# A Fourier mixing layer and a capacity-limited mixture of experts on one core: row gathers in another order with a third buffer, running sums in PSUM, scatters declared independent, two selection rounds fewer, and loads on another queue

## The chip, the cores and the metric

One core of a Trainium2 chip. The metric is device time in microseconds (us) of one execution; of several executions the median is given. Engines: TensorE (PE: matmuls; PEld: its weight loads), VectorE (DVE), ScalarE (ACT), GpSimd (POOL) and SyncE (SP). SP, ScalarE and GpSimd each have a queue on which they issue DMAs.

## The reference

```python
# x: 8 x 2496 x 256; w_r, w_i: 256 x 256; 8 experts, capacity 80
X = np.fft.rfft(x, axis=1)
Yr = Xr @ w_r - Xi @ w_i + b_r
Yi = Xr @ w_i + Xi @ w_r + b_i
Yr = np.sign(Yr) * np.maximum(np.abs(Yr) - 0.01, 0.0)      # Yi the same
y = np.fft.irfft(Yr + 1j * Yi, n=2496, axis=1)
...
x = y.reshape(19968, 256)
expert_idx = np.argmax(x @ w_gate, axis=1)
gate_w = softmax(x @ w_gate)[np.arange(N), expert_idx]
for e in range(8):
    tok_idx = ...   # the 80 tokens of expert e with the largest gate_w
    h = np.maximum(x[tok_idx] @ w1[e], 0.0)                 # w1: 256 x 1024
    out[tok_idx] = gate_w[tok_idx, None] * (h @ w2[e])      # w2: 1024 x 256
```

All other rows of the 19968 x 256 output are zero.

## The kernel before

The transform over 2496 = 39 x 64 positions is done in two steps, 39-point (stage A) and 64-point (stage B), for each of 8 batches. Stage A's results z leave PSUM as a high half in fp16 (ScalarE, L325) and a low half (VectorE, L326), are stored to DRAM (SP, L333) and come back in another layout (SP, loadZ, L363). Stage B (L374 to L376) multiplies z by the table t2s; its results go through the complex weights (L432) and the soft threshold, then back through the 64-point transform. The last step of the inverse is not completed for all tokens: its inputs are stored to DRAM as two tables of rows, `hd[0]` and `hd[1]`. A shorter path computes the gate values of all tokens from them.

At the start of the program, batch 0's x comes in three chunks (L279). While stage A of batch 0 goes over its six parts q, ScalarE's queue issues, behind q = 0, the load of t2s (L1391) and of w_r and w_i (`loadC`, L206), and behind q = 1 the three pieces of batch 1's x (`x1`). Before stage B, TensorE runs 44 matmuls on zeros (L1400) that only keep it at work.

The choice of tokens (`level2`, `rounds`) holds for each expert a list of candidates on one partition and takes the largest eight in each round: a MAX8 (L947), their places by FIND_INDEX8 (L953) and their removal by MATCH_REPLACE8 (L955). The list of the old batches ("b") goes through 80 / 8 = 10 rounds while the last batch is still worked on; it is later merged with the last batch's list of 48 (`NEW`). `choose` turns the result into `posA`, the 640 places, as five groups of 128.

From there on the tail (`experts`) completes 128 chosen tokens per group g:
- `begin` and `gather_h` fetch by GpSimd (L1085) the token ids (`tok`), 13 rows of 256 numbers per token in two parts (`hx0` of 7 rows, `hx1` of 6 rows) and 13 weights (`wv`). `hx0`, `hx1` and `wv` have two buffers each. Weights of expert 7 take `hx` buffers in turn when the groups are done with them (SP, L816); ScalarE (L833), GpSimd (L844) and VectorE (L842) split these into a high and a low half.
- `position` forms the weighted sum y of the 13 rows. For groups 0 and 1 TensorE does rows 6 and 10 to 12, or 10 to 12, through diagonal matrices D that VectorE builds from `wv` (L1140), and VectorE the others (L1148). For groups 2 to 4 ScalarE scales five (four in group 3) rows, of which GpSimd adds up z (L1159), and VectorE adds the other rows into y (L1162); y + z ends it (L1163).
- `columnsY` transposes y on TensorE (L1188 together with the D sums, L1192), and ScalarE and VectorE take it out of PSUM as xT, high and low half (L1195, L1196).
- `ffn1` (L1209) and `ffn2` (L1224) are the two layers of each expert on its 80 columns; hp, the hidden values, leave PSUM by L1211 and L1212.
- `give` transposes the finished columns (L1229), scales them by `gateA` (ScalarE, `og`, L1231) and scatters 128 rows to the output (GpSimd, L1232) at the rows `sidA`, five times in all.

`rows` computes `gateA` and `sidA` on VectorE. `busy` gives TensorE matmuls whose results nobody reads (L1175). `behind(...)` and `issue_after` order an instruction after another on its own engine. PSUM of the tail is a pool of two slots of 1024 numbers for y and the transposes (`pc`) and four of 512 (`pf`).

## Time and profile before

| | |
|---|---|
| median of 3 runs | 595.74 us (594.79 to 597.72) |
| the profiled execution | 593.25 us |
| its span, first to last instruction | 591.0 us |
| mean granted TensorE clock | 0.957 |
| busy: PE, DVE, ACT, POOL | 533.2, 400.6, 324.1, 369.2 us |
| DMA | 136.95 MB, mean 232 GB/s over the span |
| issued by GpSimd (q0, software) | 2128 packets, 9.25 MB, 4.8% of 16 engines |
| issued by ScalarE (q10) | 4262 packets, 8.79 MB, 4.9% |

The profile is one execution. Rows of a timeline give start, duration, engine, line, operation, output and inputs; `x7` stands for seven in a row. What stands in brackets is the idle time of the engine just ahead and the instruction that released it; "issue" means that the profile shows no wait. TensorE's clock is granted at one of two levels, 1.2 or 2.4 GHz, and a stretch's figure is the mean as a share of 2.4 GHz. Matmul ends are modelled.

### The profile page before, as it was taken

How to read it: one execution, taken by the hardware profiler on the slowest of the kernel's cores; microseconds unless marked ns; L12 is line 12 of the kernel's file. 1: busy time of each engine (PE TensorE's matmuls, PEld its weight loads, DVE VectorE, ACT ScalarE, POOL GpSimd, SP SyncE). 2: the span in 40 equal slices, each digit the busy share in tenths (PEclk: the TensorE clock that was granted, in tenths of full speed). 3: DMA queues.
4: the chain of work that ended last, by engine and by line, in shares of the span. 5: the costliest groups of instructions: out<-in, count | busy, mean ns of one | idle time of the engine just before them, and what ended most of it. 6: DMA issues, size and time to landing. Idle time of an engine off the chain costs nothing. (4 is left out here: it accounts for less than half of the span.)

```text
span 591.0 us, 12924 instructions
## 1 busy us (share of the span) xinstructions
PE 533.2 (90%) x5048; PEld 386.2 (65%) x5048; DVE 400.6 (68%) x778; ACT 324.1 (55%) x466; POOL 369.2 (62%) x288
## 2 busy tenths in 40 slices
PE   7969999999999999999999899988899988976792
PEld 3356676668677776877686568756667865445792
DVE  4423556666766767666777977798999676944970
ACT  2225778575756756575666556554745466302561
POOL 2005887686867777786778656676972297173681
PEclk9979999999999999999999999989999967988897
DMA  7788898987989689888979766989847797468530
GB/s 229 238 235 232 298 221 271 267 280 199 279 271 319 173 262 266 282 240 255 294 220 289 226 185 174 298 244 304 209 136 205 186 297 252 127 206 270 197 100 32
DMA packets 97571, 136.95 MB, mean 232 GB/s; under 512 B 26564, under 2 KB 78412, under 8 KB 95750
## 3 DMA queue, kind: packets, MB, share of 16 engines
q1 hardware_dynamic: 91115, 118.03, 69.0%
q10 hardware_dynamic: 4262, 8.79, 4.9%
q0 software_dynamic: 2128, 9.25, 4.8%
q8 instruction: 41, 0.67, 0.5%
q14 instruction: 25, 0.20, 0.1%
HBM read 70.75 MB, written 65.29 MB: 230 GB/s over the span
## 5 line engine op out<-in xcount | busy, mean ns | idle before, releaser
L432 PE MATMUL ps<-XT,WM 128*128 128x288 f16 (+4 forms) x1536 | 218.8, 299 | 11.0 <-DVE R L461 5.5
L432 PEld LDWEIGHTS <-WM 128*128 128x128 f16 x1536 | 149.9, 99 | 69.7 <-issue 11.0
L461 DVE SCALAR_TENSOR_TENSOR R<-ps,thr,tp 128x674 f32<-128x674 f32 (+1 forms) x56 | 48.6, 867 | 71.5 <-ACT tp L456 67.8
L479 POOL TENSOR_TENSOR YT<-R,YT 128x1408 f16<-128x1408 f32 (+1 forms) x28 | 73.5, 2624 | 31.6 <-ACT YT L478 29.9
L456 ACT ACTIVATE tp<-ps,thr 128x674 f32<-128x674 f32 (+1 forms) x56 | 43.6, 778 | 85.1 <-PE ps L432 85.1
L464 POOL TENSOR_TENSOR R<-R,sgs 128x576 f32<-128x576 f32 x28 | 35.9, 1281 | 76.1 <-DVE R L461 73.4
L291 POOL TENSOR_TENSOR xs<-xt,xs 117x1024 f16<-117x1024 f32 (+1 forms) x39 | 76.3, 1957 | 9.9 <-ACT xs L290 9.8
L374 PE MATMUL ps<-t2s,z 128*128 128x128 f16 x320 | 57.9, 222 | 7.9 <-DMA z<-zs 6.5
L326 DVE TENSOR_TENSOR zs<-ps,zs 128x1024 f16<-128x1024 f32 (+1 forms) x45 | 51.1, 1135 | 20.3 <-ACT zs L325 20.0
L380 DVE TENSOR_TENSOR XT<-ps,XT 128x640 f16<-128x640 f32 (+2 forms) x64 | 51.5, 814 | 13.4 <-ACT XT L379 12.8
L379 ACT ACTIVATE XT<-ps 128x640 f16<-128x640 f32 (+2 forms) x64 | 44.5, 701 | 24.5 <-PE ps L376 23.2
L375 PE MATMUL ps<-t2s,z 128*128 128x128 f16 x320 | 57.9, 222 | 0.0
L376 PE MATMUL ps<-t2s,z 128*128 128x128 f16 x320 | 57.8, 222 | 0.0
L305 PE MATMUL ps<-xs,t1s 117*128 117x512 f16 x213 | 52.5, 379 | 1.0 <-POOL xs L291 0.8
L325 ACT ACTIVATE zs<-ps 128x1024 f16<-128x1024 f32 (+1 forms) x45 | 43.0, 955 | 14.1 <-PE ps L305 7.0
L547 DVE TENSOR_TENSOR YO<-ps,YO 128x768 f16<-128x768 f32 (+1 forms) x50 | 45.4, 907 | 6.3 <-ACT YO L546 6.3
L589 PE MATMUL ps<-YO,vqs 128*128 128x512 f16 (+1 forms) x252 | 48.1, 331 | 0.0
L478 ACT ACTIVATE YT<-R 128x1408 f16<-128x1408 f32 (+1 forms) x28 | 35.5, 1267 | 21.5 <-POOL R L475 21.4
L535 PE MATMUL ps<-wgi,YT 128*128 128x144 f16 (+1 forms) x302 | 43.5, 229 | 3.5 <-DVE R L461 1.3
L536 PE MATMUL ps<-wgi,YT 128*128 128x136 f16 (+1 forms) x302 | 42.7, 225 | 0.0
L546 ACT ACTIVATE YO<-ps 128x768 f16<-128x768 f32 (+1 forms) x50 | 38.5, 775 | 3.1 <-PE ps L536 1.7
L589 PEld LDWEIGHTS <-vqs 128*128 128x128 f16 x252 | 24.4, 99 | 21.6 <-issue 1.0
(321 smaller groups left out, 998.1 us busy)
## 6 DMA issues: line engine op xcount, KB each, us to landing
out<-zero SPq DMA_DIRECT2D x48, 384.0 KB
hd<-hs SPq DMA_DIRECT2D x94, 192.0 KB
z<-zs SPq DMA_DIRECT2D x35, 512.0 KB
xt<-in_x SPq DMA_DIRECT2D x41, 312.0 KB
z<-z SPq DMA_DIRECT2D x14, 528.0 KB
pair<-in_moe_w SPq DMA_DIRECT2D x12, 512.0 KB
z<-z SPq DMA_DIRECT2D x14, 432.0 KB
wt<-in_moe_w ACTq DMA_DIRECT2D x10, 512.0 KB
```

The lines of the kernel that those rows point to most:

```text
L291: nc.gpsimd.tensor_tensor(xs[:, 1, :ng], xt[:, j0:j0 + ng], xs[:, 0, :ng], op=ALU.subtract)
L305: nc.tensor.matmul(pt[:, 512 * j:512 * j + 512], t1s[:, t], xs[:, h, 2 * j:2 * j + 2], start=(i == 0), stop=(i == 2))
L326: evD.append(nc.vector.tensor_tensor(zs[:, :ng, 1, :], pv[:, :ng], zs[:, :ng, 0, :], op=ALU.subtract))
L374: nc.tensor.matmul(o, zz(0), t2s[:, cl, 0, :], start=True, stop=False)
L375: nc.tensor.matmul(o, zz(0), t2s[:, cl, 1, :], start=False, stop=False)
L376: nc.tensor.matmul(o, zz(1), t2s[:, cl, 0, :], start=False, stop=True)
L380: nc.vector.tensor_tensor(ov(1), pv, ov(0), op=ALU.subtract)
L432: nc.tensor.matmul(pt[:, o:o + e - a], WM[:, dh, m, wh, 128 * eh:128 * eh + 128], XT[:, dh, xh, c, a:e], start=(i == 0), stop=(i == len(te ...
L461: nc.vector.scalar_tensor_tensor(fv(Rf), pv, thr[:, eh, ri, 1:2], fv(t), op0=ALU.add, op1=ALU.min)
L479: nc.gpsimd.tensor_tensor(yv(1), rv, yv(0), op=ALU.subtract)
L547: dvs.append(nc.vector.tensor_tensor(yol, yy, yoh, op=ALU.subtract))
L589: nc.tensor.matmul(o, tab[:, v], yo(h), start=(i == 0), stop=(i == 2))
```

## The change

1. The loads of t2s, w_r, w_i and of batch 1's first chunk are issued by GpSimd instead of ScalarE. Ahead of each of the two sets GpSimd copies one number of stage A's low half (q = 0, q = 1) to `junk`, so that the loads are issued after these. 34 instead of 44 matmuls keep TensorE at work ahead of stage B.
2. The list of the old batches goes through 64 / 8 = 8 rounds; its tail is filled by two memsets, and the largest value left out (`m`) takes the last chosen one in, by one more maximum.
3. In the tail the gathers have another order, `hx0` and `wv` a third buffer, and gathers are issued three groups ahead. `gateA` is computed ahead of the diagonal matrices, `sidA` later. The running sums of groups 2 to 4 lie in one PSUM tile `yp`, and the final y + z goes to SBUF; these sums are ordered behind the y of the group before. PSUM is one slot (`pc`), one bank for the transposes of groups 2 to 4 (`pct`), one for `yp` and four of 512. TensorE's unread matmuls are 16 ahead of the gathers and 6 behind, in place of 27.
4. The scatters are declared not to depend on each other. In a branch that is not taken here the dependence is written out by hand.

The diff's core:

```diff
+OLD = 64
...
-            pin(nc.scalar.dma_start(wt, w.rearrange("(h p) e -> p h e", p=128)))
+            pin(nc.gpsimd.dma_start(wt, w.rearrange("(h p) e -> p h e", p=128)))
...
-                wt = p5.tile([128, 7 - i, 256], F32, name=f"hx{i}", bufs=2)...
+                wt = p5.tile([128, 7 - i, 256], F32, name=f"hx{i}", bufs=3 - i)...
...
+        if nm == "b":
+            lists = [const.tile([8, CAP], dt, name=f"t{k}b") for k, dt in enumerate((F32, U32))]
+            nc.gpsimd.memset(lists[0][:, n:], -1.0)
+            nc.gpsimd.memset(lists[1][:, n:], 0)
...
+            steps.append(lambda: nc.vector.tensor_tensor(m, m, tv[:, n - 1:n], op=ALU.max))
...
-        wv = p5.tile([128, 16], F32, name="wv", bufs=2)
-        with behind((nm, "z", g - 2)):
-            gather(wv, vt, ct[:, g, 2:3], order)
+        wv = p5.tile([128, 16], F32, name="wv", bufs=3)
+        gather(wv, vt, ct[:, g, 2:3], order)
...
-            t = p5.tile([128, 7 - p, 256], F32, name=f"hx{p}", bufs=2)
-            with behind((nm, "z", g - 2)):
-                gi = gather(t.rearrange("p r e -> p (r e)"), hd[p], ct[:, g, 1:2], order)
+            t = p5.tile([128, 7 - p, 256], F32, name=f"hx{p}", bufs=3 - p)
+            gather(t.rearrange("p r e -> p (r e)"), hd[p], ct[:, g, 1:2], order)
...
-                with behind((nm, "xv", g - 1)):
+                with behind((nm, "xv", g - 1)) if g else tc.issue_after(idms[-1].ins):
                     nc.vector.tensor_tensor(D[:, i:j], ...)
...
+        yp = pyp.tile([128, 256], F32, name="yp", bufs=1)
         with behind((nm, *LATER[g][0])):
-            nc.scalar.activation(y, hx[0], AF.Copy, scale=w(0))
+            nc.scalar.activation(yp, hx[0], AF.Copy, scale=w(0))
...
-                with behind((nm, *LATER[g][1])):
-                    nc.vector.scalar_tensor_tensor(y, hx[r], w(r), y, op0=ALU.mult, op1=ALU.add)
-        nc.vector.tensor_tensor(y, y, z, op=ALU.add)
+                with behind((nm, "y", g - 1) if r < 4 else (nm, "xv", g - 1)):
+                    nc.vector.scalar_tensor_tensor(yp, hx[r], w(r), yp, op0=ALU.mult, op1=ALU.add)
+        ev[nm, "y", g] = nc.vector.tensor_tensor(y, yp, z, op=ALU.add)
...
+        for j in given:
+            tc.declare_no_dep(i.ins, j.ins, reason="a token's row is in one group alone")
+        given.append(i)
...
-        got.append(gather_h(nm, 1, ct, True, None, lambda: [get(g) for g in range(3, n)]))
+        got.append(gather_h(nm, 1, ct, True, lambda: get(3)))
+        get(4)
+        got.append(gather_h(nm, 2, ct, True))
...
-                feedX(S, PS0())
+                feedX(S, PS0() if S["f"] < 2 else pct.tile([128, 512], F32, name="pt", bufs=1))
...
+        if q < 2:
+            pin(nc.gpsimd.tensor_copy(junk, zl[-1][0:1, 0, 1, 0:1]))
         if q == 0:
-            pin(nc.scalar.dma_start(t2s[:, 0:11], t2[:, 0:11]))
+            pin(nc.gpsimd.dma_start(t2s[:, 0:11], t2[:, 0:11]))
             loadC()
         if q == 1:
-            x1 = loadX(1, 0, None, (A_, A_, A_))
+            x1 = loadX(1, 0, None, (nc.gpsimd,) * 3)
...
-    for _ in range(44):
+    for _ in range(34):
...
-                bg = level2("b", CAP, 16)
+                bg = level2("b", OLD, 16)
...
-        ps[0], ps[1] = ctx.enter_context(tc.tile_pool(name="pc", bufs=2, space=PSUM, reuse_waits="tile")), 2
+        ps[0], ps[1] = ctx.enter_context(tc.tile_pool(name="pc", bufs=1, space=PSUM, reuse_waits="tile")), 1
+        pct = ctx.enter_context(tc.tile_pool(name="pct", bufs=1, space=PSUM, reuse_waits="tile"))
+        pyp = ctx.enter_context(tc.tile_pool(name="pyp", bufs=1, space=PSUM, reuse_waits="tile"))
...
-        busy(27, pairs[6, 1][1][:, 1024:1536])
+        busy(BUSY[1], pairs[0, 0][0])
```

GpSimd at the start of the program, before (`ident` is a unit matrix, `it` a counter; the memsets of `tp` clear a border of the weights' tile and come behind w_r and w_i):

```order
L249 DMA v1h<-in_v1f 39x78
L258 ISA
L258 IOTA it 128x1
masks.py:199 AFFINE_SELECT ident<-ident 128x128
L216 MEMSET tp_143 128x30
L216 MEMSET tp_144 128x30
```

The same place after the change:

```order
masks.py:199 AFFINE_SELECT ident<-ident 128x128
L1411 COPY junk<-zs 1x1
L1413 DMA t2s<-in_t 128x2816
L208 DMA tp_143<-in_w_r 128x2x256
L208 DMA tp_144<-in_w_i 128x2x256
L1411 COPY junk<-zs 1x1
L281 DMA xt<-in_x 39x2048 x3
L218 MEMSET tp_143 128x30
L218 MEMSET tp_144 128x30
```

The six loads are new on this queue, each set behind a copy that reads stage A's `zs`. Line numbers of the changed kernel are its own: L1413, L208 and L281 are the loads of t2s, the weights and x.

GpSimd's gathers in the tail, from group 0's weights to the first sums of group 2, before (`hd_104` and `hd_105` are the tables `hd[0]` and `hd[1]`; `hx_6761`, `hx_6765` are group 0's two parts, `hx_6768`, `hx_6774` group 1's, `hx_6881`, `hx_6885` group 2's, `hx_6973`, `hx_6977` group 3's):

```order
L1085 DMA tok<-cid,posA 128x4
L1085 DMA hx_6768<-hd_104,tok 128x1792
L1085 DMA tok<-cid,posA 128x4 x2
L1085 DMA wv<-in_vt,tok 128x16
L1085 DMA hx_6774<-hd_105,tok 128x1536
L1085 DMA wv<-in_vt,tok 128x16
L1085 DMA hx_6881<-hd_104,tok 128x1792
L1085 DMA hx_6885<-hd_105,tok 128x1536
L1085 DMA hx_6973<-hd_104,tok 128x1792
L1085 DMA wv<-in_vt,tok 128x16
L1085 DMA hx_6977<-hd_105,tok 128x1536
L1159 TENSOR_TENSOR y_7199<-hx_6881,y_7199 128x256 x2
```

And after the change (group 1's parts are `hx_6781` and `hx_6786`, group 2's `hx_6789` and `hx_6793`, group 3's `hx_6879` and `hx_6883`, and `hx_6971` is group 4's first part):

```order
L1098 DMA tok<-cid,posA 128x4
L1098 DMA hx_6786<-hd_105,tok 128x1536
L1098 DMA tok<-cid,posA 128x4
L1098 DMA hx_6789<-hd_104,tok 128x1792
L1098 DMA wv<-in_vt,tok 128x16
L1098 DMA hx_6793<-hd_105,tok 128x1536
L1098 DMA hx_6879<-hd_104,tok 128x1792
L1098 DMA wv<-in_vt,tok 128x16
L1098 DMA hx_6971<-hd_104,tok 128x1792
L1098 DMA hx_6883<-hd_105,tok 128x1536
L1098 DMA wv<-in_vt,tok 128x16
L1169 TENSOR_TENSOR y_7197<-hx_6789,y_7197 128x256 x2
```

Group 1's second part and group 2's first part each stand one gather nearer to the start, and group 4's first part and weights stand ahead of the sums (L1159, now L1169) and not behind them.

VectorE between the choice of tokens and group 0's sums, before (`wt` holds the matrices D of group 0, `ff` and `flag` say whether the branch is taken):

```order
L1029 TENSOR_TENSOR fl<-t2b,th 8x1
L1140 TENSOR_TENSOR wt<-ident,wv 128x128
L1140 TENSOR_TENSOR wt<-ident,wv 128x384
L1148 SCALAR_TENSOR_TENSOR y<-hx_6761,wv,y 128x256
L1148 SCALAR_TENSOR_TENSOR y_6868<-hx_6761,wv,y_6868 128x256
L1148 SCALAR_TENSOR_TENSOR y<-hx_6761,wv,y 128x256
L1148 SCALAR_TENSOR_TENSOR y_6868<-hx_6761,wv,y_6868 128x256
L1148 SCALAR_TENSOR_TENSOR y<-hx_6765,wv,y 128x256
L1148 SCALAR_TENSOR_TENSOR y_6868<-hx_6765,wv,y_6868 128x256
L1148 SCALAR_TENSOR_TENSOR y<-hx_6765,wv,y 128x256
L1248 TENSOR_SCALAR gateA<-ps 128x5
L1149 TENSOR_TENSOR y<-y,y_6868 128x256
```

And after the change:

```order
L1042 TENSOR_TENSOR fl<-t2b,th 8x1
L1264 TENSOR_SCALAR gateA<-ps 128x5
L1266 TENSOR_SCALAR idmA<-gateA 128x5
L1046 TENSOR_REDUCE ff<-ps 1x1
L1148 TENSOR_TENSOR wt<-ident,wv 128x128
L1148 TENSOR_TENSOR wt<-ident,wv 128x384
L1047 CAST flag<-ff 1x1
L1156 SCALAR_TENSOR_TENSOR y<-hx_6774,wv,y 128x256
L1156 SCALAR_TENSOR_TENSOR y_6866<-hx_6774,wv,y_6866 128x256
L1156 SCALAR_TENSOR_TENSOR y<-hx_6774,wv,y 128x256
```

`gateA`, with `idmA` and `ff`, went from behind the seven sums (L1148, now L1156) to ahead of the matrices D (L1140, now L1148).

## Rows read from the trace of the kernel before

**Rows 1.** The page, busy time and share of the span of TensorE, then its weight loads.
```profile
PE 533.2 (90%) x5048; PEld 386.2 (65%) x5048; DVE 400.6 (68%) x778; ACT 324.1 (55%) x466; POOL 369.2 (62%) x288
```

**Rows 2.** Busy time of each engine by stretch; columns in the first line.
```profile
core 0: us, PE busy (x) PEld busy (x) DVE busy (x) ACT busy (x) POOL busy (x), PEclk, DMA share, GB/s
...
20.00:30.00 10.00, 8.85 (x42) 3.84 (x40) 3.97 (x12) 1.08 (x3) 0.25 (x2) 1.00 0.69 187
...
35.00:40.00 5.00, 4.63 (x59) 4.67 (x60) 1.18 (x2) 1.85 (x3) 0.00 (x0) 0.67 0.91 217
40.00:480.00 440.00, 421.67 (x3899) 308.97 (x3897) 315.55 (x532) 268.94 (x368) 304.15 (x222) 0.98 0.85 246
...
545.00:581.00 36.00, 30.91 (x688) 29.34 (x687) 27.32 (x44) 21.55 (x51) 22.79 (x21) 0.91 0.44 142
```

**Rows 3.** TensorE's waits, 40 to 480 us: us in total, times, longest.
```profile
PE ps L432 <- DVE R L461: 5.5, 6, 2.7
```

**Rows 4.** The chain that ended last, in order of time: start, us, what.
```profile
579.58 3.55 DMA out<-og,sidA
```

**Rows 5.** Timeline of ScalarE and its queue, 5 to 40 us.
```profile
12.15 4.51 ACTq L279 DMA_DIRECT2D xt<-in_x  x3
16.71 1.02 ACT L325 ACTIVATE zs<-ps 128x1024 f16<-128x1024 f32 x1 [5.34 <-DMA xt<-in_x]
```

**Rows 6.** Timeline of TensorE, 5 to 40 us.
```profile
12.17 3.70 PE L307 MATMUL ps<-xt,t1f 117*128 117x512 f32 x8 [1.87 <-DMA xt<-in_x]
15.71 2.74 PE L307 MATMUL ps<-XT,t1f 117*128 117x512 f32 x6
19.04 9.66 PE L1400 MATMUL ps<-z 128*128 128x512 f16 x44 [0.60 <-DVE zs L326]
...
35.37 0.27 PE L374 MATMUL ps<-t2s,z 128*128 128x128 f16 x1 [6.51 <-DMA z<-zs]
```

**Rows 7.** Timeline of VectorE, 5 to 40 us.
```profile
18.91 2.94 DVE L326 TENSOR_TENSOR YO<-ps,YO 128x1024 f16<-128x1024 f32 x3
```

**Rows 8.** Timeline of VectorE, 479 to 490 us.
```profile
482.91 0.66 DVE L955 MATCH_REPLACE8 V<-t0b,V 8x512 f32<-8x512 f32 x1
...
483.83 0.67 DVE L947 MAX8 t0b<-V 8x8 f32<-8x512 f32 x1
...
485.69 0.67 DVE L953 FIND_INDEX8 t1b<-t0b,V 8x8 uint32<-8x512 f32 x1
...
488.14 0.67 DVE L747 COPY hs<-ps 39x512 f32<-39x512 f32 x1
```

**Rows 9.** Timeline of TensorE, 479 to 492 us.
```profile
489.46 0.36 PE L783 MATMUL ps<-ident,Gs 78*128 78x78 f32 x1 [3.43 <-DVE Gs L777]
```

**Rows 10.** Timeline of TensorE, 528 to 581 us.
```profile
530.39 2.05 PE L1188 MATMUL ps<-wt,hx 128*128 128x128 f32 x16 [1.36 <-DVE gateA L1248]
...
553.59 0.44 PE L1192 MATMUL ps<-ident,y 128*128 128x128 f32 x2 [0.94 <-DVE y L1163]
...
559.57 0.41 PE L1192 MATMUL ps<-ident,y 128*128 128x128 f32 x2 [1.47 <-DVE y L1163]
```

**Rows 11.** Timeline of GpSimd, 515 to 591 us.
```profile
540.33 0.94 POOL L1085 DMA_INDIRECT hx<-hd,tok  x1 [2.81 <-ACT hp L1211]
541.58 0.95 POOL L1085 DMA_INDIRECT wv<-in_vt,tok  x1 [0.30 <-issue]
...
567.26 4.59 POOL L844 TENSOR_TENSOR pair<-hx,pair 128x1024 bf16<-128x1024 f32 x2
...
583.90 0.98 POOL L1232 DMA_INDIRECT out<-og,sidA  x1 [3.33 <-DMA out<-og,sidA]
```

**Rows 12.** VectorE, 515 to 591 us, by line and form: count, busy us, mean ns.
```profile
L1162 DVE SCALAR_TENSOR_TENSOR y<-hx,wv,y 128x256 f32<-128x256 f32 x22 | 16.9, 775 | 0.5
L1212 DVE SCALAR_TENSOR_TENSOR hp<-pf,hp 128x320 f16<-128x320 f32 x16 | 7.5, 483 | 2.3 <-ACT hp L1211 2.3
L1148 DVE SCALAR_TENSOR_TENSOR y<-hx,wv,y 128x256 f32<-128x256 f32 x15 | 6.4, 478 | 0.1
```

**Rows 13.** Timeline of ScalarE, 560 to 591 us.
```profile
581.06 0.47 ACT L1231 ACTIVATE og<-ps,gateA 128x256 f32<-128x256 f32 x1 [0.58 <-PE ps L1229]
```

More of the change, by code (lines that the diff above doesn't have):

```diff
@@ L313, in fourier_mix_then_moe @@
     evD = []
+    zl = []
     junk = const.tile([1, 1], F16, name="junk")
@@ L1177, in fourier_mix_then_moe @@
     warms = []
+    BUSY = (16, 6)
     def columnsY(nm, g, y, xT, pt):
@@ L1278, in experts @@
     def experts(S, n, gate, sid):
-        given = 0
+        done = 0
         hps = {}
@@ L1298, in last @@
         def last(e):
-            nonlocal given
-            while 128 * (given + 1) <= n * e:
-                give(S["nm"], given, oT, gate, sid, PS1())
-                given += 1
+            nonlocal done
+            while 128 * (done + 1) <= n * e:
+                give(S["nm"], done, oT, gate, sid, PS1())
+                done += 1
         first(0)
@@ L1659, in fourier_mix_then_moe @@
         for g in range(NG):
-            nc.gpsimd.indirect_dma_start(out=out, out_offset=bass.IndirectOffsetOnAxis(ap=sidA[:, g:g + 1], axis=0),
-                                         in_=zero[:, 0], in_offset=None, bounds_check=B * S - 1, oob_is_err=False)
+            i = nc.gpsimd.indirect_dma_start(out=out, out_offset=bass.IndirectOffsetOnAxis(ap=sidA[:, g:g + 1], axis=0),
+                                             in_=zero[:, 0], in_offset=None, bounds_check=B * S - 1, oob_is_err=False)
+            for j in given:
+                tc.add_manual_dep(i.ins, j.ins.name, mybir.DependencyInfo(mybir.DependencyClass.Sync, mybir.DependencyReason.DATA), reason="the rows are written again")
+        given.clear()
         tv = slow_select()
```

52 lines of the change are left out of this document (31 added, 21 removed).

## The prediction

> **What bounds the kernel now.** I read the page first: TensorE is busy for 533.2 of the 591.0 us of span, and no other engine comes near it [rows 1]. So only what lets TensorE start earlier, wait less or run at the higher clock can move the time, and whatever stands behind TensorE's last instruction. Then the busy times by stretch: from 40 to 480 us TensorE is at work in 421.67 of 440 us, with a granted clock of 0.98 of the full 2.4 GHz [rows 2]. The list of TensorE's waits in that stretch has only other engines as releasers, the largest sum 5.5 us in six waits, and no DMA [rows 3]. An earlier start of that stretch is therefore carried through it, and an edit has to be priced at the two ends: the first 35 us, and from 480 us on. There the rows show TensorE waiting, and the reader is to look at what released it each time. The chain that ended last starts only with the fourth scatter's transfer: the last scatter on GpSimd's queue was released by that transfer [rows 4], not by the data that it scatters.
>
> All sums are made against the profiled execution, 593.25 us (span 591.0 and 2.25 around it). The median of the three runs is 595.74, 2.49 more; I add that at the end.
>
> **The start.** Six loads leave ScalarE's queue for GpSimd's: t2s, w_r, w_i and the three pieces of batch 1; by their shapes 704, 256, 256 and three times 312 KB. Before, the three pieces held ScalarE's sequencer for 4.51 us from 12.15, and the third copy of stage A out of PSUM began only at 16.71 after 5.34 us of idle time [rows 5]. Its matmuls were done long before: eight of them, for two of these copies, began at 12.17 and took 3.70 us [rows 6], so the first four were done at about 14.0 (half of 3.70 is 1.85). The copy can start some 2.7 us earlier. TensorE's 1.87 us wait for x ahead of those eight [rows 6] may shrink too, since 1.2 MB of t2s and w no longer run ahead of x. On the other side, the last low halves need TensorE's last six matmuls, which ended at 18.45; two copies and a subtraction behind that, VectorE is done near 20.5 instead of at 18.91 + 2.94 = 21.85 [rows 7]. From there the way goes over the stores of z to DRAM and its loads back to stage B's first matmul at 35.37, which waited 6.51 us for z [rows 6]. The DMA engines were busy for only 0.69 of 20 to 30 us [rows 2], so there is room: earlier stores find free engines. Bounds: 0 (the transfers take the time back), and 2.7 + 1.87 = 4.5 us. I take **-2.2**, between VectorE's 1.4 and ScalarE's 2.7, and nearer the latter because the third store is issued behind the copy that was late. The moved loads cost GpSimd nothing: in the old order nothing but a memset of w's tile, which has to wait for w anyway, stands there. Ten warm-up matmuls fewer (44 took 9.66 us, so 10 are 2.2 us) cost nothing if they end that much earlier before the same wait; stage B's first stretch runs at a clock of 0.67 in the 35 to 40 us row already [rows 2], so the fall at that place is not new.
>
> **The selection.** Two rounds of the old list go. In VectorE's timeline four of their instructions stand ahead of the copy L747: L955 twice, 0.66 each, L947 and L953, 0.67 each [rows 8], 2.66 us together; the rest comes behind it. VectorE is without a gap there, and TensorE waits 3.43 us for the result of L777, just behind that copy [rows 9]. So the removal lies on the path, and is smaller than the wait. Spacing from start to start is nearer 0.6 than 0.66 us, and an 8x1 maximum is added, so I take **-2.3**. Bounds: 0, if what follows waits for the stores of hd instead, and -4, if TensorE's shorter wait also spares it part of the half clock behind it. The two memsets that pad the list stand in GpSimd's idle start. A weight copy on ScalarE and two weight loads on SP come later; expert 7's aside, their use lies tens of us off.
>
> **The tail, gate first.** gateA goes ahead of the build of D on VectorE. Before, TensorE's first row sums of group 0 waited 1.36 us for gateA, which stood behind the seven sums [rows 10]. Now they wait for D and the gathered halves only. The chain to xT of group 0, and through it to group 1's sums, moves by that: **-1.3**, between 0 (they wait for the second gather instead) and -2.5 (the whole two us of row sums go beside VectorE's). Fewer warm-ups (26 for 31) are cover that is lost; see the slower rival.
>
> **Gathers.** Group 1's second half and group 2's first half are issued one gather earlier, group 4's first half ahead of GpSimd's sums of group 2, and the third buffer takes the wait for a free one from the first halves of groups 2 and, in part, 3; one takes 0.95 us of GpSimd and 0.30 of its queue [rows 11]. Group 1's sums stood behind xT of group 0, and those of groups 2 to 4 were fetched while TensorE was on experts 0 to 3. The one long wait on GpSimd, 2.81 us ahead of group 3's first half [rows 11], held nothing up but itself. I cost this at 0: the cover is the sums of the group before. If the cover is gone, a group's landing decides, one gather, 1.25 us, per group. GpSimd's own sums of group 2 now stand behind two more gathers on that queue, 2.5 us of issue that fills idle time such as this 2.81 us.
>
> **Sums in PSUM.** 22 sums of groups 2 to 4 ran at 775 ns each; 15 of the same form for groups 0 and 1, when GpSimd added nothing beside them, at 478 ns; a similar instruction with one operand in PSUM and 320 instead of 256 elements took 483 ns all through the tail [rows 12]. With the running sum in PSUM I take 478 ns: 22 x 0.297 = 6.5 us less of VectorE. What of it is on the path is read from TensorE's waits for the finished y: 0.94 and 1.47 us [rows 10], and some 0.7 behind them for xT. Against it stands that one PSUM tile takes the groups one after the other and VectorE may no longer begin group 3 beside group 2; but group 2's sums alone, seven of 0.48, are 3.4 us. I take **-1.7**; bounds 0 and -3.2.
>
> [...]
>
> **Last scatter.** og of the last group is ready at 581.06 + 0.47 = 581.53 [rows 13]; the scatter started at 583.90 after 3.33 us of waiting for the fourth's transfer [rows 11]. Without that wait it can start some 0.2 to 0.3 us after og: **-2.1**, bounds -1.5 and -2.4. What follows, its landing and the end of the program, stays.
>
> **Sum.** -2.2 - 2.3 - 1.3 - 1.7 - 2.1 = -9.6. 593.25 - 9.6 = 583.65; with 2.49, **586.1 us** as a median.
>
> **Rivals.** (a) The start is not carried: the moved loads run beside the stores of z, 2.15 MB in all, and stage B starts where it did. For: DMA busy shares near 1 around it. Against: the 0.69 row. 588.3. (b) Expert 7's weights become the bound: GpSimd's last two copies of them ran until 567.26 + 4.59 = 571.85 [rows 11], just ahead of their use, and the gate's and the sums' 3.0 us are lost. Against: their buffers come free with group 4's sums, which end earlier too. 589.1. (c) Start, selection, gate and sums are all swallowed, by landings of hd ahead of the gathers and by the weights; only the scatter is left. 593.6, no change. (d) The scatters still wait for each other's landing in another way, so the change does not do what it says there: 588.2. (e) **Slower**: TensorE's clock. It falls to 1.2 GHz behind its waits; in the 36 us from 545 the mean is 0.91 with 30.91 us of work [rows 2]. With fewer warm-ups and one PSUM slot for transposes, it could wait oftener and stay low. 1 us of work at full clock costs 1 us more at half, so the gains are gone, and 3 us more, when 12.6 us of the tail's work run at half clock that ran at full: the mean of that stretch would have to fall to about 0.67. Then 598.7. Against: the waits that I see there get shorter. (f) Better than forecast: start -4.5, selection -4, sums -3.2: 593.25 - 15.1 + 2.49 = 580.6.
>
> **How the numbers follow.** The forecast 0.43, (a) 0.15, (b) 0.12, (c) 0.10, (d) 0.04, (e) 0.06, (f) 0.10. About 0.5%, 3 us, is what a measurement of this kernel can tell from no change. Faster by more: all but (c) and (e), 0.84; the same: (c), 0.10; slower: (e), 0.06. The range leaves out (c), (e) and the far end of (f): 578 to 592.5.
>
> **What would show it.** In the changed profile: ScalarE's third copy of stage A near 14, not 16.7; stage B's first matmul near 33; VectorE's copy L747 some 2.3 us nearer to stage B's end, and TensorE's wait behind it about 1 us; TensorE's first row sums of group 0 released by D or a gather; the 22 sums near 0.48 us; the last scatter released by og. I am wrong if stage B starts at 35 or later, if the sums stay above 0.7 us, or if TensorE's clock in the last 36 us falls well below 0.9.

## The result, and the profile after

The changed kernel takes 588.51 us as a median of four runs (588.24 to 590.94); four runs of the kernel before beside it gave 596.73 (594.79 to 598.71). The ratio is 0.9875 [0.984, 0.9911], 7.5 us less. Ratios and their intervals, here and below, leave out executions more than 1.5% above the fastest of the same kernel (three of the kernel before, one of f4), while medians hold all. The profiled execution took 588.24 us, its span is 586.4. It is the shortest of its four, and before's profiled one, 593.25 us, is shorter than any of the four beside it; the two traces differ by only 4.6 us of span, and the further traces below serve to tell what belongs to the change.

The page of the changed kernel, busy time and share of the span of each engine, answers to [rows 1]:

```profile
PE 532.3 (91%) x5033; PEld 388.1 (66%) x5033; DVE 391.7 (67%) x769; ACT 324.3 (55%) x466; POOL 372.7 (64%) x298
```

TensorE's work is the same within 1 us; VectorE has 8.9 us less. Busy times by stretch, changed kernel, answering to [rows 2]:

```profile
core 0: us, PE busy (x) PEld busy (x) DVE busy (x) ACT busy (x) POOL busy (x), PEclk, DMA share, GB/s
...
35.00:40.00 5.00, 5.00 (x52) 5.00 (x51) 1.71 (x2) 1.68 (x3) 0.00 (x0) 0.53 0.90 198
...
524.00:535.00 11.00, 9.17 (x74) 8.52 (x75) 6.13 (x17) 1.58 (x5) 8.69 (x8) 0.53 0.79 261
545.00:577.00 32.00, 28.54 (x686) 27.34 (x682) 20.13 (x44) 20.35 (x49) 19.30 (x19) 0.95 0.36 123
```

Two clocks are lower than before: 0.53 for 0.67 at 35 to 40 us, and 0.53 at 524 to 535, where before's trace has 1.00:

```profile
524.00:535.00 11.00, 7.53 (x49) 4.80 (x47) 4.79 (x16) 0.91 (x2) 7.05 (x8) 1.00 0.81 272
```

The last 32 us are better, 0.95 for the 0.91 of [rows 2]. The records of the clock in both traces are all 0.50 or 1.00; a stretch has their mean. In before's trace it is 0.50 from 520 to 522 us, where the unread matmuls of 512 columns (L1175) start 0.427 us apart, 1.2 columns a ns, and 1.00 from 523 to 525, where they start 0.216 us apart, 2.4 columns a ns; at one column a clock, an estimate from these spacings, that is 1.2 and 2.4 GHz.

The start, timeline of TensorE, answering to [rows 6] (start, us, instruction, in brackets the idle time ahead and its releaser):

```profile
12.94 3.70 PE L309 MATMUL ps<-xt,t1f 117*128 117x512 f32 x8 [2.13 <-DMA xt<-in_x]
...
19.06 7.50 PE L1422 MATMUL ps<-z 128*128 128x512 f16 x34
...
34.35 0.29 PE L378 MATMUL ps<-t2s,z 128*128 128x128 f16 x1 [7.64 <-DMA z<-zs]
```

And ScalarE's third copy, which stood at 16.71 behind the load [rows 5]:

```profile
14.96 1.02 ACT L328 ACTIVATE zs<-ps 128x1024 f16<-128x1024 f32 x1 [3.10 <-PE ps L309]
```

It now waits for the matmuls only, and those began 0.77 us later, since x itself landed later. Stage B starts 1.02 us earlier.

At the other end, TensorE's timeline of the selection and the tail, answering to [rows 9, 10]:

```profile
488.38 0.29 PE L786 MATMUL ps<-ident,Gs 78*128 78x78 f32 x1 [1.27 <-DVE Gs L780]
...
523.84 0.74 PE L1200 MATMUL ps<-wt,hx 128*128 128x128 f32 x4 [2.25 <-DVE wt L1148]
525.62 2.90 PE L1200 MATMUL ps<-wt,hx 128*128 128x128 f32 x12 [1.04 <-DMA hx<-hd,tok]
...
535.35 0.72 PE L1200 MATMUL ps<-v3s,hx 128*128 128x128 f32 x5 [0.46 <-issue]
536.78 0.36 PE L1200 MATMUL ps<-v3s,hx 128*128 128x128 f32 x1 [0.71 <-issue]
538.21 0.36 PE L1236 MATMUL pf<-hp,pair 128*128 128x80 f16 x3 [1.03 <-DVE y L1156]
538.92 0.23 PE L1236 MATMUL pf<-hp,pair 128*128 128x80 f16 x1 [0.36 <-issue]
539.62 0.85 PE L1236 MATMUL pf<-hp,pair 128*128 128x80 f16 x8 [0.47 <-issue]
...
550.53 0.44 PE L1204 MATMUL pt<-ident,y 128*128 128x128 f32 x2 [0.16 <-DVE y L1174]
...
556.68 0.41 PE L1204 MATMUL pt<-ident,y 128*128 128x128 f32 x2 [1.60 <-DVE y L1174]
```

The wait behind the selection's copy is 1.27 instead of 3.43 us; the row sums of group 0 are released by D and a gather, not by gateA; of the waits for y, the first has gone from 0.94 to 0.16, the second is as long as it was. New are the stops from 535 to 540 us, which no releaser explains; the last section returns to them. VectorE by lines and forms, 508 to 587 us (count, busy us, mean ns, idle before), answering to [rows 12]:

```profile
L1173 DVE SCALAR_TENSOR_TENSOR yp<-hx,wv,yp 128x256 f32<-128x256 f32 x22 | 10.7, 487 | 1.1 <-ACT yp L1161 0.6
...
L1156 DVE SCALAR_TENSOR_TENSOR y<-hx,wv,y 128x256 f32<-128x256 f32 x15 | 6.4, 472 | 0.0
```

The 22 sums take 487 instead of 775 ns. The last two scatters on GpSimd's queue, answering to [rows 11]:

```profile
576.02 0.98 POOL L1244 DMA_INDIRECT out<-og,sidA  x1 [6.78 <-ACT og L1243]
578.25 0.98 POOL L1244 DMA_INDIRECT out<-og,sidA  x1 [1.25 <-ACT og L1243]
```

The last one is released by og, not by the fourth's transfer.

To place the difference, five points were read from the timelines of every trace: B, stage B's first matmul (L378, in before L374); C, the first matmul of the complex weights (L435, L432); P, the start of posA (L1261, L1243); X, ScalarE's xT of group 0 (L1207, L1195); T, the end of TensorE's last instruction; and the span's end. Set 1 holds d1 to d4, set 2 e1 to e4, set 3 f1 to f4, each set on one chip, all compared with runs of the kernel before on that chip.

| trace | B | C | C to P | P to X | X to T | T to end | span |
|---|---|---|---|---|---|---|---|
| before | 35.37 | 40.41 | 474.86 | 20.06 | 45.65 | 10.06 | 591.03 |
| changed | 34.35 | 40.58 | 471.75 | 17.13 | 47.96 | 8.98 | 586.40 |
| f1 (before again) | 36.47 | 41.77 | 475.69 | 17.70 | 44.65 | 9.63 | 589.44 |
| e1 (changed again) | 34.27 | 40.81 | 471.60 | 17.27 | 41.37 | 9.00 | 580.05 |
| f2 (changed again) | 35.12 | 41.04 | 471.85 | 17.18 | 43.72 | 9.12 | 582.92 |
| e4 (64 warm-ups) | 34.39 | 38.09 | 474.58 | 16.61 | 41.33 | 9.11 | 579.72 |
| e2 (old gathers) | 34.35 | 40.58 | 471.50 | 17.14 | 46.19 | 8.71 | 584.12 |
| f3 (old gathers and sums) | 35.03 | 40.94 | 474.79 | 17.71 | 44.48 | 8.72 | 586.64 |
| d3 (old sums) | 33.86 | 39.97 | 472.26 | 17.16 | 52.03 | 9.04 | 590.46 |
| d4 (scatters wait) | 34.42 | 40.03 | 474.50 | 19.21 | 46.40 | 12.67 | 592.81 |
| d1 (old start) | 36.14 | 41.60 | 470.39 | 20.58 | 46.47 | 8.31 | 587.36 |
| d2 (ten rounds) | 33.87 | 39.91 | 475.97 | 20.58 | 44.91 | 8.80 | 590.17 |
| e3 (idf late) | 35.56 | 40.89 | 474.21 | 17.40 | 41.09 | 9.07 | 582.67 |
| f4 (old start, ten rounds) | 37.64 | 43.23 | 474.26 | 17.21 | 42.63 | 8.19 | 585.52 |

In the first pair, the gain lies in the stretch from C to P (3.1 us), in P to X (2.9) and behind T (1.1), and X to T gives 2.3 us back. The traces of sets 2 and 3 say something else of the last two stretches, which is why those sets were needed.

### The profile page after: what moved, and what is told of

Read it like the earlier page. It is cut to its first block, busy times and chain, and to the rows that moved or that the text cites. A ratio compares the mean times of both kernels' runs of the same rounds, so it can differ in the third digit from the quotient of the medians.

```text
span 586.4 us, 12894 instructions
## 1 busy us (share of the span) xinstructions
PE 532.3 (91%) x5033; PEld 388.1 (66%) x5033; DVE 391.7 (67%) x769; ACT 324.3 (55%) x466; POOL 372.7 (64%) x298
## 4 chain that ended last, share of the span: by engine, by line
PE 47%; DVE 17%; DMA 8%; issue 8%; ACT 7%; POOL 7%; SPq 2%; another core or an unknown queue 1%; DVEq 0%; POOLq 0%; ACTq 0%
PE ps L435 23%; PE ps L307 6%; PE ps L592 4%; DVE R L464 2%; PE ps L630 2%; ACT tp L459 2%; DVE YO L550 2%; PE ps L567 1%; DMA xt<-in_x 1%; PE ps L378 1%; PE ps L538 1%; PE ps L379 1%; PE ps L380 1%; DVE XT L384 1%
## 5 line engine op out<-in xcount | busy, mean ns | idle before, releaser
L435 PE MATMUL ps<-XT,WM 128*128 128x288 f16 (+4 forms) x1536 | 219.0, 300 | 10.0 <-DVE R L464 4.7
L435 PEld LDWEIGHTS <-WM 128*128 128x128 f16 x1536 | 150.1, 99 | 68.6 <-issue 9.9
L378 PE MATMUL ps<-t2s,z 128*128 128x128 f16 x320 | 59.0, 224 | 10.9 <-DMA z<-zs 7.6
L379 PE MATMUL ps<-t2s,z 128*128 128x128 f16 x320 | 59.0, 224 | 0.0
L380 PE MATMUL ps<-t2s,z 128*128 128x128 f16 x320 | 59.0, 224 | 0.0
```

Of the source, the lines that this page charges most:

```text
L378: nc.tensor.matmul(o, zz(0), t2s[:, cl, 0, :], start=True, stop=False)
L379: nc.tensor.matmul(o, zz(0), t2s[:, cl, 1, :], start=False, stop=False)
L380: nc.tensor.matmul(o, zz(1), t2s[:, cl, 0, :], start=False, stop=True)
L435: nc.tensor.matmul(pt[:, o:o + e - a], WM[:, dh, m, wh, 128 * eh:128 * eh + 128], XT[:, dh, xh, c, a:e], start=(i == 0), stop=(i == len(te ...
```

## The experiments

The edits are to the changed kernel unless said otherwise. The first set takes back one part each.

**d1, the start as before.**

```diff
-            pin(nc.gpsimd.tensor_copy(junk, zl[-1][0:1, 0, 1, 0:1]))
-            pin(nc.gpsimd.dma_start(t2s[:, 0:11], t2[:, 0:11]))
+            pin(nc.scalar.dma_start(t2s[:, 0:11], t2[:, 0:11]))
...
-    for _ in range(34):
+    for _ in range(44):
```

(w_r, w_i and batch 1's pieces go back to ScalarE too.)

> The changed kernel with the start as before: the six loads on ScalarE's queue, no copies to junk, 44 warm-up matmuls. Theory (the start's gain is taken back by TensorE's clock: the changed trace has stage B 1.02 us earlier and the first L435 0.17 us later): stage B starts at 35.2 to 35.6 us and runs at the higher clock from about 38, the first matmul with the complex weights within 0.4 us of the changed kernel's 40.6, and the median is that of the changed kernel, 588 to 589. Rival (the start is worth about what was predicted, and the one trace hides it): median 590 to 591.5.

Measured: 591.61 us, ratio 0.9925 [0.9893, 0.9958] to the kernel before. B stands at 36.14 and C at 41.60, later than in the changed kernel by 1.8 and 1.0 us. The part is worth something, but less at C than at B. The theory (the median of the changed kernel, C within 0.4 us) missed; the rival's 590 to 591.5 is nearer. In its one trace nothing of the loss is left at the choice of tokens: posA starts at 511.99 (41.60 + 470.39), in the changed kernel at 512.33.

**d2, ten rounds of the selection.**

```diff
-                bg = level2("b", OLD, 16)
+                bg = level2("b", CAP, 16)
```

(without the two memsets and the added maximum)

> The changed kernel with ten rounds for the old lists again (80, no padding, no extra maximum). Theory (the selection's whole 2.8 us lie on the path): posA's result near 515, the copy behind the rounds near 488, median 591 to 592. Rival (group 1's stall behind the gathers ends at about the same time whenever the gathers start, so what comes earlier is waited for there): posA 2.5 us later than in the changed kernel, group 1's xT at most 1 us later, median 588.5 to 589.5.

Measured: 591.71 us, 0.9941 [0.9914, 0.9967], as the theory had it, with posA at 515.88.

**d3, the running sums in SBUF again.**

```diff
-        yp = pyp.tile([128, 256], F32, name="yp", bufs=1)
+        yp = y
```

> The changed kernel with the running sums of groups 2 to 4 in SBUF (yp is y), in the changed order. Theory (PSUM spares VectorE the meeting with GpSimd): the 22 sums take 0.7 to 0.85 us each again instead of 0.487, TensorE waits longer for y of groups 2 and 3, median 590 to 592. Rival (it was the new order that made them fast, since no group's sums are mixed with the next group's): 0.5 us each, median within 0.5 us of the changed kernel.

Measured: 595.1 us, 0.9993 [0.9971, 1.0014]: without this one line nothing of the gain is left, more than the 590 to 592 us of the theory. VectorE by lines of d3, and TensorE's longest wait for y in its timeline:

```profile
L1173 DVE SCALAR_TENSOR_TENSOR y<-hx,wv,y 128x256 f32<-128x256 f32 x22 | 16.2, 734 | 0.6
```

```profile
559.84 0.41 PE L1204 MATMUL pt<-ident,y 128*128 128x128 f32 x2 [3.54 <-DVE y L1174]
```

22 times 247 ns are 5.4 us of VectorE, and the wait for y is 3.54 us where the changed kernel has 1.60. The mean of 734 ns is of two prices. The first five sums of group 2 on VectorE and the additions on GpSimd beside them, in d3 and then in the changed kernel:

```profile
544.89 3.64 DVE L1173 SCALAR_TENSOR_TENSOR y<-hx,wv,y 128x256 f32<-128x256 f32 x5
545.73 4.08 POOL L1169 TENSOR_TENSOR y<-hx,y 128x256 f32<-128x256 f32 x5 [1.51 <-ACT hx L1166]
```

```profile
545.08 2.59 DVE L1173 SCALAR_TENSOR_TENSOR yp<-hx,wv,yp 128x256 f32<-128x256 f32 x5
545.95 3.86 POOL L1169 TENSOR_TENSOR y<-hx,y 128x256 f32<-128x256 f32 x5 [1.52 <-ACT hx L1166]
```

One by one, the eight of d3's 22 with no addition of GpSimd beside them take 478 to 485 ns, most of the others 830 to 845, and one beside a split of 1024 elements 2239. In the changed kernel all 22 take 480 to 490 ns, 14 of them with a GpSimd addition or split beside them for more than half of their time.

**d4, the scatters wait for each other.**

```diff
-        for j in given:
-            tc.declare_no_dep(i.ins, j.ins, reason="a token's row is in one group alone")
```

> The changed kernel with the scatters in order behind each other's landing, as before. Theory (2.1 us of wait for the last scatter, of which 1.05 us are given back because the program's end came 1.05 us later behind the last scatter): the fifth scatter starts 3.2 to 3.6 us behind the fourth's end, the end comes 7.1 us behind its start, median 589.3 to 590. Rival (the later end has another cause): the end is 8.1 us behind the last scatter, median 590.4 to 591.

Measured: 592.56 us, 0.9945 [0.992, 0.997]. GpSimd's timeline in d4:

```profile
583.04 0.98 POOL L1244 DMA_INDIRECT out<-og,sidA  x1 [3.31 <-DMA out<-og,sidA]
```

The wait of [rows 11] is back, and with it 3.7 us behind TensorE's end (12.67 against 8.98). Both expectations missed: the end comes 9.8 us behind the last scatter's start, not 7.1 or 8.1, and the median is 1.6 us above the rival's range.

Against 0.9875 the four undone parts cost 0.0050, 0.0066, 0.0118 and 0.0070, together 18.1 us of 595.78, more than twice the gain. Either the parts lean on each other, or the chip of this set differs from the one of the first pair. So the next sets carry the changed kernel as a control.

**e1 and f2, the changed kernel again; f1, the kernel before again.** No edit.

> The changed kernel once more, as the control of this set: the four runs before it scatter more than its own first four. All theories: a ratio near 0.988 to 0.99. If it is above 0.992, the first measurement was lucky and every difference is to be read against this one.

> The changed kernel, as the control of this set. Ratio 0.984 to 0.991 by the two earlier measurements.

> The kernel before, unchanged, for its trace on the chip of this set (the chips differ: 595.8 us in one set, 590.8 in the other). Theory (TensorE's stops in steps of 0.7 us belong to a chip, not to the change): if the control of this set has no such stops, neither has this one, and group 0's and group 1's xT lie 17 to 18 and 26 to 28 us behind posA instead of 20.1 and 29.7; ratio 1 within 0.3%. Rival (the kernel before always has them): 20 and 29.7 again.

Measured: e1 581.5 us against 590.82, 0.9855 [0.9806, 0.9903]; f2 582.36 against 590.51, 0.9832 [0.9783, 0.9881]; f1 591.07, 0.9994 [0.9957, 1.003]. The change is worth 8.6 and 9.9 us there by the ratios, 9.3 and 8.2 by the medians, and neither trace of the changed kernel has the stops of 535 to 540 us. e1's TensorE in the same place:

```profile
533.59 2.35 PE L1200 MATMUL ps<-v3s,hx 128*128 128x128 f32 x12
...
535.78 1.88 PE L1236 MATMUL pf<-hp,pair 128*128 128x80 f16 x48
```

**e2, the gathers as before.** The old order, two buffers of `hx0` and `wv`, gathers two groups ahead and behind the sum of two groups earlier; the sums stay in PSUM.

```diff
-            if g + 3 < S["n"]:
-                S["got"].append(gather_h(S["nm"], g + 3, S["ct"]))
+            if g + 2 < S["n"]:
+                S["got"].append(gather_h(S["nm"], g + 2, S["ct"]))
...
-        wv = p5.tile([128, 16], F32, name="wv", bufs=3)
-        gather(wv, vt, ct[:, g, 2:3], order)
+        wv = p5.tile([128, 16], F32, name="wv", bufs=2)
+        with behind((nm, "z", g - 2)):
+            gather(wv, vt, ct[:, g, 2:3], order)
```

> The changed kernel with the gathers as before: two buffers, the old order, two groups ahead, each waiting for GpSimd's sums two groups back; all else as changed. In five traces of the new order group 1's xT comes 32 to 32.7 us behind posA (48.4 - 15.9 and so on), though group 0's xT comes 17 to 20.6 behind it; before it was 29.7, with group 0's at 20.1. Theory (the three-deep gathers crowd the DMA engines from 18 to 29 us behind posA, and TensorE and ScalarE stand still in that stretch): group 1's xT at 27 to 30 behind posA, no steps of 0.7 us in TensorE's starts, median 1.5 to 3 us below the changed kernel's. Rival (group 1 is late because VectorE's order puts idf ahead of its sums and because TensorE runs at half clock): still 31.5 to 32.7 behind posA, median as the changed kernel's or 1 us above it, since groups 2 and 3 come later.

Measured: 587.91 us, 0.9962 [0.9937, 0.9986]; to e1's ratio that is 6.3 us of 590.82. The theory, 1.5 to 3 us below the changed kernel, missed by sign, the rival, at most 1 us above it, by size. The part that the sum had at nothing takes most of the gain with it. ScalarE's timeline in e2:

```profile
552.76 1.06 ACT L836 ACTIVATE pair<-hx 128x1024 f16<-128x1024 f32 x1 [3.58 <-DMA hx<-in_moe_w]
553.73 0.37 ACT L1209 ACTIVATE xT<-pt 128x256 f16<-128x256 f32 x1
```

L836 splits a piece of expert 7's weights, L1209 makes xT of group 3 and stands behind it in ScalarE's order. The piece is loaded into a buffer of the gathered rows (`hx`), and it comes 3.58 us late. TensorE's timeline:

```profile
550.49 0.41 PE L1206 MATMUL pt<-ident,y 128*128 128x128 f32 x2 [1.64 <-DVE y L1176]
...
554.14 0.29 PE L1223 MATMUL pf<-xT,pair 128*128 128x80 f16 x2 [3.25 <-ACT xT L1209]
```

In the control, ScalarE's and then TensorE's rows for the same group:

```profile
548.82 1.05 ACT L836 ACTIVATE pair<-hx 128x1024 f16<-128x1024 f32 x1
...
551.04 0.38 ACT L1207 ACTIVATE xT<-pt 128x256 f16<-128x256 f32 x1 [0.98 <-PE pt L1204]
```

```profile
550.59 0.41 PE L1204 MATMUL pt<-ident,y 128*128 128x128 f32 x2 [1.63 <-DVE y L1174]
551.47 0.23 PE L1221 MATMUL pf<-xT,pair 128*128 128x80 f16 x2 [0.47 <-ACT xT L1207]
```

The transposes start at the same time, the work behind them 2.67 us earlier, because the weights' piece is there at 548.82. SP's queue shows why: the first load of expert 7 is issued 5.94 us later in e2 (first row) than in the control (second), at 547.38 during group 3's sums and not at 541.44 during group 2's, since with two buffers of `hx0` group 4's rows take group 2's and the weights have to wait for group 3's.

```profile
547.38 12.66 SPq L819 DMA_DIRECT2D hx<-in_moe_w  x4
```

```profile
541.44 16.09 SPq L819 DMA_DIRECT2D hx<-in_moe_w  x4
```

Group 4 is late in e2 as well, and not by its gathers: the last of them has landed at 551.28, and VectorE starts the group's sums at 554.49, behind xT of group 3. Its y then waits for GpSimd's last addition, which stands behind a split of expert 7 (L847):

```profile
561.12 2.13 POOL L847 TENSOR_TENSOR pair<-hx,pair 128x1024 bf16<-128x1024 f32 x1 [0.79 <-ACT pair L836]
```

```profile
563.97 0.42 DVE L1176 TENSOR_TENSOR y<-yp,y 128x256 f32<-128x256 f32 x1 [1.44 <-POOL y L1171]
```

This is one profile of e2; the size is from twelve runs. e2 takes back the order, the depth and the buffers at once, so that what the order alone is worth is not shown.

**f3, gathers and sums as before.** The edits of e2 and d3 together.

> The changed kernel with both the gathers as before (two buffers) and the running sums in SBUF. Alone, each of the two brought the ratio to 0.996 (gathers) and 0.999 (sums). Theory (each needs the other: early rows are of use only to fast sums, and fast sums only with early rows, so either one undone loses the gain of both): ratio 0.995 to 1.001, no worse than the sums alone; group 4's xT 34 to 36 us behind group 0's, as in the kernel before (35.1). Rival (two separate gains of 6 and 7 us): 1.006 to 1.012.

Measured: 586.35 us, 0.993 [0.9909, 0.9951], a little below the theory's 0.995 to 1.001 and far from the rival's 1.006: 0.0098 from f2's ratio, 5.8 us (4.0 by the medians). So the two parts are not additive: undoing the sums costs 7.0 us (d3, on another chip and against the first pair's ratio), the gathers 6.3, both 5.8. By itself, as far as ratios from three chips can be set side by side, either of them brings nothing; e2, which has the PSUM sums alone, is if anything worse than f3, which has neither. f3's ScalarE has its first split of expert 7 at 559.78, behind xT of group 3 (557.11): with slower sums that xT is ordered ahead of the weights, and their lateness is hidden. TensorE waits in f3 for the sums instead:

```profile
556.66 0.41 PE L1206 MATMUL pt<-ident,y 128*128 128x128 f32 x2 [2.64 <-DVE y L1176]
```

**f4, start and selection as before.** The edits of d1 and d2 together.

> The changed kernel with the start as before and ten rounds of selection, only the tail changed. Theory (the start's 1 us is carried to 335 us and lost at the two places behind it, where waits for DMA set the pace, so only the selection's 2.5 to 3 us count): 2.5 to 3.5 us above the control of this set. Rival (both count, as their runs alone seemed to say, 3 us each): 5.5 to 7 us above it.

Measured: 586.15 us, 0.987 [0.9806, 0.9934]; 2.2 us above f2 by the ratios, whose intervals overlap, and 2.7 by the medians of the executions that enter them. That is the theory's region, not the rival's 5.5 to 7, but zero is not excluded.

**e3, the conversion for `sidA` later.** In the changed kernel VectorE's L1268 waited 1.6 us for a list of indices ahead of group 1's sums. It goes behind group 1's y.

```diff
+            with behind((nm, "y", 1)):
+                nc.vector.tensor_copy(idf, S["ct"][:, :, 0])
+                nc.vector.tensor_tensor(sidA, idm, idf, op=ALU.add)
```

> The changed kernel with idf and sidA behind group 1's y on VectorE (they waited 1.60 us for a gather of ids ahead of group 1's sums). Theory of the gathers: no change in group 1's xT, 32 to 32.7 behind posA, because ScalarE's hp at 27.4 comes later anyway; median within 1 us of the changed kernel's. Rival (idf): group 1's xT 1.5 us earlier, median 1 to 1.6 us lower.

Measured: 583.39 us, 0.9859 [0.9815, 0.9903], the control's ratio, and group 1's xT 25.6 us behind posA, e1 25.8. That wait was not on the path.

**e4, 64 warm-up matmuls.**

```diff
-    for _ in range(34):
+    for _ in range(64):
```

> The changed kernel with 64 instead of 34 matmuls ahead of stage B, 30 more by 0.22 us, 6.6 us, so that TensorE is at work until about 33 us. Theory (the clock's fall in the 7.6 us of waiting took back the start's gain): no half clock in stage B's first stretch, the first matmul with the complex weights at 37.5 to 38.5 instead of 40.6, and those 2 to 3 us carried to posA and into the median. Rival (from 40 us on a DMA or another engine sets the pace): the same first matmul, but less than 1 us of it at 440 us and in the median.

Measured: 583.74 us, 0.9876 [0.9832, 0.9921], no gain: 2.7 us would be 0.0046 less than e1's ratio, and this one is 0.0021 more (the two intervals together give 0.0066 either way). Locally it does what it should. TensorE's timeline of e4:

```profile
18.71 13.98 PE L1422 MATMUL ps<-z 128*128 128x512 f16 x64
...
34.39 0.23 PE L378 MATMUL ps<-t2s,z 128*128 128x128 f16 x1 [1.55 <-DMA z<-zs]
...
336.51 4.95 PE L435 MATMUL ps<-XT,WM 128*128 128x337 f16 x24 [2.74 <-DVE R L464]
```

Stage B's first matmul takes 0.23 instead of 0.29 us, the granted clock of 35 to 40 us is 1.00, and C comes at 38.09, 2.7 us before e1's. The lead still stands at 336.51, where e1 is at 338.96 (2.45 us). There e1 draws nearer by the clock that TensorE gets behind the same wait. e1's row:

```profile
338.96 3.64 PE L435 MATMUL ps<-XT,WM 128*128 128x337 f16 x24 [2.73 <-DVE R L464]
```

The same 24 matmuls take 3.64 us in e1, at a granted clock of 1.00, and 4.95 in e4, at 0.72. e1 is the exception: in the 12 other traces they take 5.08 to 5.30 behind the same wait. So e4 is better compared with the first trace of the changed kernel, where they run from 338.83 and take 5.30. Behind them e4 is 2.67 us ahead, at the third stage's wgm matmuls (L676; 465.72 against 467.12) 1.40, and at posA (512.67 against 512.33) 0.34 behind. The chain that ended last in the changed kernel shows what may pace these stretches (start, us, what):

```profile
375.27 4.21 DMA hd<-hs
397.47 6.66 DMA out<-zero
...
464.69 3.93 DMA gd<-gh
...
477.51 6.20 DMA wt<-in_moe_w
```

Stores, loads of expert weights and a store of zeros stand on the chain, one step behind the engines that release TensorE. That they used up the lead is an argument from this chain; no run takes them away.

No version beat the changed kernel: e3 and e4 lie within its interval.

## Why the prediction held, and where it did not

586.1 us was forecast and 588.51 measured: the sum had 9.6 us, the ratio gives 7.5 (8.6 and 9.9 in the two controls). The sum is near, but its terms are not the ones that made it, and that they add up to nearly the same is in part luck. The number alone decides nothing either: rivals (a), (b) and (d), at 588.3, 589.1 and 588.2, lie nearer to 588.51 than the forecast. The table's means are taken over all traces with or without a part, from single executions; where a part is undone by itself, the runs have the say.

- **The start, forecast -2.2.** The mechanism is as told: the third copy moved from 16.71 to 14.96. TensorE's wait for x ahead of it did not shrink but went from 1.87 to 2.13. B is at 36.4 in the four traces with the old start and at 34.5 in the ten with the new one, -1.9, close to the term, though still later than the 33 that was named; in three of the ten (35.03, 35.12, 35.56) it is at 35 or later, which the text had as a sign of being wrong. At C only -1.2 is left (41.75 against 40.53 without e4). The step that failed is that ten warm-up matmuls fewer "cost nothing if they end that much earlier before the same wait": the wait grew from 6.51 to 7.64 us in the first pair, and the clock of the row behind it (35 to 40 us) fell from 0.67 to 0.53. e4, where the wait is 1.55, has 1.00 there; e1 and d1, with waits of 5.73 and 6.50, have 0.50 and 0.51, so the length of the wait alone does not set it. "An earlier start of that stretch is therefore carried through it" does not hold for e4, whose 2.7 us are not in the median: that no DMA releases TensorE there [rows 3] says nothing of the DMAs that may hold up the engines that do. For the start itself it stays open, since the wgm matmuls come at 468.6 in the four traces with the old start and at 467.2 in the ten with the new one. Rival (a) had its result partly right, for another reason.
- **The selection, forecast -2.3.** VectorE's copy now starts behind 0.62 us of idle time for TensorE, where it had no gap before:

```profile
487.14 0.68 DVE L750 COPY hs<-ps 39x512 f32<-39x512 f32 x1 [0.62 <-PE ps L748]
```

  So VectorE was more than caught up, and the end of the gain is set by TensorE. The half clock behind the wait, which the bound of -4 names, is in before's trace (0.50 from 489.46 to 492 us, behind 3.43 us of waiting); behind the 1.27 us of the changed kernel it is 0.86 (488.38 to 491). C to P is 3.1 us shorter in the first pair, and 3.8 and 4.1 in f2 and e1 against f1, but d4, e3 and f3, which have the part, show little or no gain there; by the runs, d2's 3.9 us rest on the ratio of the first pair, and f4's 2.2 to 2.7 hold the start too. The sign stands by the traces (means below), the size lies between 1 and 4 us.
- **The gate, forecast -1.3.** In P to X the kernel before again shows 17.70 and the controls 17.27 and 17.18: -0.5. TensorE now waits 2.25 us for D, which waits for the gathered weights, and 1.04 for the second gather: the bound that the text put at 0 took most of it. before's 20.06 is not a measure of this part: f1, on a chip without the stops, does not have it, and d1 and d2, with the part, show 20.58. No run takes the gate back by itself, and only f1 shows its absence undisturbed.
- **Sums in PSUM, forecast -1.7, and gathers, forecast 0.** The price of a sum was right: 487 ns, where 478 was taken. Together the two parts bring 2.6 us of X to T (44.65 in f1; 42.0 as the mean of e1, f2, e3, e4 and f4), and 4.0 by the medians of f3 and f2 or 5.8 by their ratios. What failed is the step "I cost this at 0: the cover is the sums of the group before". It priced a gather by its landing alone, while the worth that e2's trace shows lies in the third buffer: without it the weights of expert 7 come later, and sums that are a third shorter no longer hide that. This is the mechanism of rival (b), and e2 shows it in the kernel that lacks the third buffer. Against (b) the text said that these buffers come free with group 4's sums; for the first of them it is group 2's with three buffers (541.44 in e1) and group 3's with two (547.38 in e2). The text weighed each part with the others left in place, and so could not see it.
- **The price of a sum by where it lies.** In the changed kernel's trace a sum takes 487 ns with the running sum in PSUM (L1173) and 472 with it in SBUF (L1156), 15 ns less. The likely reason why the sums were slow before lies in d3's two prices in SBUF: 478 to 485 ns without a GpSimd addition beside them, most of the others 830 to 845. With the running sum in PSUM the price is 480 to 490 ns, with GpSimd at work beside it or not. The slow sums are those with an addition beside them; what in the hardware couples the two engines, no row shows.
- **The last scatter, forecast -2.1.** og of the last group ends at 577.51 + 0.47 = 577.98, and the scatter starts 0.27 us behind it, as forecast. But from TensorE's end to the span's end there is only 1.0 us less (9.85 in before and f1, 8.82 as the mean of the eleven traces without d4). "What follows, its landing and the end of the program, stays" failed: from the last scatter's start to the end it is 591.03 - 583.90 = 7.1 us before and 586.40 - 578.25 = 8.1 after. That goes with the start's part and hardly with this one: d1 and f4, with free scatters and the old start, have 7.5 and 7.4 there, f1 has 7.5, and the nine traces with free scatters and the new start have 7.9 to 8.3. Taken so, the scatters are worth 1.6 us (9.85 against 8.25 in d1 and f4), just inside the term's bounds, and the new start costs 0.7 at the end, a term that the sum lacks; how it does so is open. Within the changed kernel the part is worth 3.7 us by the trace and 4.2 by d4's runs; d4's end behind its last scatter is 9.8 us, for which no row gives a reason. One reading of the prediction is off, without weight for the sum: the chain of [rows 4] begins with the third scatter's transfer, at 575.27, not the fourth's.
- **The slower rival (e).** The clock did fall where warm-ups were cut: 524 to 535 us at 0.53, where before had 1.00; whether the warm-ups or the waits for D and the gathers lowered it, no run separates. The last stretch stands at 0.95. In the changed kernel's trace 46 matmuls of a first layer (L1221) take 3.23 us from 530.35, at 0.50, and 1.81 from 568.46, at 1.00. What it cost shows on the chips without stops, in the first layer of group 0, in f1 and then in e1:

```profile
536.55 1.81 PE L1209 MATMUL pf<-xT,pair 128*128 128x80 f16 x46 [0.73 <-DVE xT L1196]
```

```profile
530.57 3.23 PE L1221 MATMUL pf<-xT,pair 128*128 128x80 f16 x46 [0.17 <-DVE xT L1208]
```

  Group 1's xT comes 7.04 us behind group 0's in f1 and 8.39 as the mean of e1, f2, e3, e4 and f4. So some 1.4 us were lost there, and X to T behind group 1's xT gained 4.0, not 2.6. The rival's mechanism is there; its size, 12.6 us, is not. (c) and (d) are refuted by the ratio and by the last scatter's releaser.

With the means -1.2 (start), -0.5 (gate), -2.6 (sums and gathers), -1.0 (end) and some -1.6 for the selection (47.69 in four traces with ten rounds and 46.06 in ten with eight, from the wgm matmuls to posA) the sum is -6.9, 0.6 short of the first pair and up to 3 short of the controls. Single executions differ by 1 to 2 us in each stretch, so that this is as far as traces settle it.

## What to carry to other kernels

When a part is costed at nothing because other work covers it, ask whether another part of the same change shortens that cover, and what else takes the buffer that it frees; a faster consumer and an earlier supply may be worth nothing singly and 4 to 6 us together, which shows only if they are taken back one by one and together. That no DMA is named among the waits of the bounding engine is no proof that an earlier start is carried through (e4's 2.7 us were not); look one step further back, at what releases the releasers. And idle time ahead of a stretch had a second price here, the clock at which the stretch began: behind waits of 5.73 to 7.64 us the row of 35 to 40 us stood at 0.50 to 0.67, behind e4's 1.55 at 1.00. Where warm-ups were cut, the start's 1.9 us at B were 1.2 at C.
